# The gate's products before the pair products, their sums in the bank of the keys by values: linear attention and a balanced mixture of experts on one core

## The chip, the cores and the metric

The kernel runs on one core of a Trainium2 chip, as one launch. The metric is the device time of that core in microseconds (us). Inputs and outputs are float32 in device memory.

## The reference

An attention block without softmax (RWKV-5 form: 4 batches, 8 heads, 768 steps, 48 values a head) feeds a layer of eight experts in which every expert gets the same number of tokens.

```python
for t in range(S):
    cur = einsum('bhd,bhe->bhde', u * k_t, v_t)
    y[:, :, t] = einsum('bhd,bhde->bhe', r_t, state + cur)
    state = w * state + einsum('bhd,bhe->bhde', k_t, v_t)
x = y as (B*S, H*D) = (3072, 384)
logits = x @ w_gate                     # 8 experts
order = argsort(-logits.flatten())      # greedy: the best (token, expert) first,
                                        # at most 384 tokens an expert
out[mask_e] = relu(x[mask_e] @ w1[e]) @ w2[e]
```

## The kernel before, in words

The program has two parts: the attention (about the first 127 us) and the experts. The change lies in the attention, class `Mild`, in which the order of the work is written out by hand: each engine executes its instructions in the order in which the code issues them, and waits for another engine only where data or a buffer has to come free.

**Rounds.** The 768 steps are cut into C = 6 chunks of 128, and a unit n is one chunk of one batch, 24 units in all, batches innermost (unit n has batch n % 4 and chunk n // 4). `run` (from L619) has a loop of 24 rounds; round n issues, in this order:

- loads for later units (SP's queue, L336);
- `turn(n + 2)` (L480): TensorE turns the scaled keys and the receptances of unit n+2 (L458, tiles `kT_ps` and `rT_ps`); ScalarE copies the keys out (L475) and VectorE multiplies the receptances by powers of the decay (L477);
- `rows((n - 1,), "few")` (L607): TensorE turns the finished x of unit n-1 back into rows (L595, tile `x_ps` in the bank "few"), ScalarE copies them (L604), SP writes them to memory (L605);
- `diagonal(n + 2, ...)` (L487): ScalarE writes the diagonals of the matrices AT of unit n+2, eight multiplications, four a half (L495). In rounds 1 and 2, and in those with a gate, the second half comes later;
- in rounds 3 and 4 only, `keep(n - 1)` here; in later rounds keep belongs to `outputs`;
- `pairs(n + 1)` (L497): 16 products of keys and receptances inside the chunk (L505, 32 records in the trace, tile `g_ps`), then two masked copies by VectorE into AT (L512);
- `keys(n + 3)` (L436) and `own(n + 3)` (L442, L443): three multiplications on GpSimd (POOL);
- in rounds 4, 8, 12, 16 and 20 (`full`), `gate(n // 4 - 1, ...)`: the logits of the chunk that was just finished, for all four batches at once, and the second half of the diagonal;
- `outputs(n)` (L534): products of the receptances with the states (L545, `y_ps<-rT,states`); `keep(n)` (L514) except in the last chunk: keys by values (L524, tile `kv_ps` in the bank "counts"), which VectorE adds to the state (L529; in the first chunk it multiplies them into it, L532) and GpSimd then scales (L530); the products by AT (L545, `y_ps<-AT,vts`); in rounds with a gate `logits` (L582), which turns the sums of the gate (L585, tile `lt_ps` in "few") and copies them into LG (L586); and ScalarE's copy of the result (L564).

**The gate** (L568 to L580): for each of 4 row groups of x and each of 4 batches one product of 128 rows by 32 columns, each batch in column group 32b of one PSUM tile, `lg_ps`; 16 products, 32 records (L575). ScalarE then copies the sums to `lg` (L580). The last chunk's gate runs behind the loop (L728, L730).

**PSUM.** The eight banks are handed out by tags, one buffer each. The tags that matter: "few" is used by turn after turn of small things (x_ps, lg_ps, lt_ps, and most of the small products of the assignment); "counts" belongs in the loop to kv_ps alone. A new tile of a tag waits until every reader of the tile before has finished.

**Work placed between.** `step(n, ...)` calls pieces of the early assignment (from round 17, L886) that pick an expert with few tokens and list them before the attention is over: the list's products go to "few" too (L1201 to L1205), their sums and comparisons run on VectorE (L936 and around). None of its places in rounds with a gate is used. `chores` are constants, on VectorE and GpSimd.

The few lines of the loop that set the order around the change:

```python
                if n + 1 < N:
                    self.pairs(n + 1, lambda: step(n, "products"))
                step(n, "paired")
            if n + 3 < N:
                self.keys(n + 3)
                self.own(n + 3)
            if full:
                self.gate(n // B - 1, range(B))
                if n + 2 < N:
                    self.diagonal(n + 2, halves[1])
```

Of the kernel before, what the change touches and what calls it, by code (L numbers as in the profile page):

```python
# [10 lines left out]
F32 = mybir.dt.float32  # L11
# [10 lines left out]
T = 128  # L22
# [4 lines left out]
def attention_any(ctx, tc, r, k, v, w, u, wg, x_dram, LG, ident, walk):  # L27
# [237 lines left out]
    for n in range(len(units)):  # L265
        if n + 1 < len(units):
            scale(n + 1)
        pairs(n)
        if n > 0:
            gate(n - 1)  # L270
        outputs(n)
    gate(len(units) - 1)


class Mild:
# [292 lines left out]
    def gate(self, c, bs):  # L568
        nc, HP, B = self.nc, self.HP, self.B
        if c not in self.lgs:  # L570
            self.lgs[c] = self.walk.ps.tile([128, T], F32, name="lg_ps", tag="few")
        lg_ps = self.lgs[c]
        for o in range(HP):
            for b in bs:
                nc.tensor.matmul(lg_ps[32 * b:32 * b + 32, :], self.wgp[:, o, :], self.xts[c * B + b][:, o, :],  # L575
                                 start=(o == 0), stop=(o == HP - 1), skip_group_check=True,
                                 tile_position=(0, 32 * b))
        if B - 1 in bs:
            self.lg = lg = self.pool.tile([128, T], F32, name="lg", bufs=1)
            nc.scalar.copy(lg, lg_ps)  # L580
# [38 lines left out]
    def run(self, step):  # L619
        N, B, C, walk = self.N, self.B, self.C, self.walk  # L620
        self.live = {n: {} for n in range(N)}
        self.start()
        u_ps = self.spread_u()
        self.again_one(0, 0)
        k0 = self.keys_turned(0, True)
        self.again_one(0, 1)
        self.idle(2, "g_ps")
        r0 = self.r_turned(0)
        self.copy_u(u_ps)
        self.own(0)  # L630
        self.scaled(0, "k", k0, "pieces")
        self.scaled(0, "r", r0, "pieces")
        self.table(self.WK, "k")
        self.again_one(1, 0)
        self.table(self.WR, "r")
        self.again_one(1, 1)
        self.idle(2, "g_ps")
        k1 = self.keys_turned(1, True, walk.ps, "few")
        wk_ps = self.wk_turned()
        r1 = self.r_turned(1, walk.ps, "counts")  # L640
        self.wk_table(wk_ps)
        self.scaled(1, "k", k1, self.WK)
        self.own_sum(0)
        self.diagonal(0, (0,))
        self.again_one(2, 0)
        self.diagonal(0, (1,))
        self.again_one(2, 1)
        self.scaled(1, "r", r1, self.WR)
        self.own(1)
        self.keys(0)  # L650
        self.own_sum(1)
        nc, AB = self.nc, self.ones8
        nc.vector.tensor_mul(self.chunk, AB[:, 0, :, 1, 8], AB[:, 0, :, 1, 8])
        self.pairs(0)
        self.diagonal(1)
        self.own(2)
        chores = walk.constants()
        for n in range(N):
            self.load(n + 5, "kr")
            self.load(n + 4, "v")  # L660
            if n == 2:
                self.gate_weights()
            soon, split, full = n <= B, 0 < n < 3, n >= B and n % B == 0
            halves = ((0,), (1,)) if split or full else ((0, 1), ())
            if n == 0:
                self.turn(2, True)
                self.own_sum(2)
                self.idle(3, "y_ps")
                self.pairs(1)
                self.keys(1)  # L670
            else:
                step(n, "first")
                if not soon and n + 3 < N:
                    self.again(n + 3)
                if n == 2:
                    self.own_sum(n + 2)
                if split:
                    self.keep(n - 1)
                    self.pairs(n + 1)
                if n + 2 < N:  # L680
                    if n != 2 and n + 3 < N:
                        self.own_sum(n + 2)
                    self.turn(n + 2, between=lambda: step(n, "turning"))
                if n <= N - B:
                    self.rows((n - 1,), "few")
            if soon:
                self.again_one(n + 3, 0)
            if n + 2 < N:
                self.diagonal(n + 2, halves[0])
            if soon:  # L690
                self.again_one(n + 3, 1)
            if n > 2:
                step(n, "turned")
                if n <= B:
                    self.keep(n - 1)
                if n + 1 < N:
                    self.pairs(n + 1, lambda: step(n, "products"))
                step(n, "paired")
            if n + 3 < N:
                self.keys(n + 3)  # L700
                self.own(n + 3)
                if n == 1:
                    self.keys(2)
            if full:
                self.gate(n // B - 1, range(B))
                if n + 2 < N:
                    self.diagonal(n + 2, halves[1])
            if n == N - 1:
                rows = self.rows_turned((N - 4, N - 3), "g_ps", lambda: step(n, "rows"))
                self.rows_out((N - 4, N - 3), rows)  # L710
            self.outputs(n, lambda: step(n, "states"), (lambda: self.logits(n // B - 1)) if full else (lambda: None))
            if split:
                self.diagonal(n + 2, halves[1])
            if n == N - 4:
                self.own_sum(N - 1)
            step(n, "last")
            if n == 13:
                walk.guess_most(self.LG[:, 0:3 * B, :], AX.XY)
            if n == 14:
                walk.guess(walk.ps.tile([128, 128], F32, name="most_ps", tag="few"), self.ident)  # L720
            if n == N // 2 + 1:
                for _ in chores:
                    pass
                self.test()
            if n > 2:
                for _ in range(6):
                    next(chores, None)
        self.gate(C - 1, range(B - 1))  # L728
        one = self.rows_turned((N - 2,), "kT_ps")
        self.gate(C - 1, [B - 1])  # L730
        last = self.rows_turned((N - 1,), "g_ps")
        self.logits(C - 1)
        return one, last
# [1285 lines left out]
```

## Time and profile before

| | us |
|---|---|
| median of 3 runs | 394.56 (394.26 to 394.99) |
| the profiled execution, time | 393.36 |
| the profiled execution, span from first to last instruction | 391.6 |
| TensorE busy (matmul) | 377.2 |
| VectorE busy | 281.4 |
| ScalarE busy | 169.3 |
| GpSimd busy | 141.2 |

All rows come from that one profiled execution. PE is the matmul stream of TensorE, PEld its weight loads, DVE VectorE, ACT ScalarE, POOL GpSimd, SP the queue that issues loads and stores. A busy time of PE is modelled at its ends, so steps on PE are read here from the start of one group to the start of the next. In a timeline row the first number is the start of a group of like instructions, the second the time from the first one's start to the last one's end. What stands in brackets at the end is idle time of that engine just before the row, and who ended it; "issue" means that nothing which the profile shows was waited for.

### The profile page before, as it was taken

The page shows a single profiled execution, that of the slowest core. Times are in us where ns is not written, and L with a number is a line of the kernel's source. Part 1 is how long each engine was busy: PE and PEld are TensorE (multiplying, and loading weights), DVE is VectorE, ACT ScalarE, POOL GpSimd, SP SyncE. Part 2 cuts the span into 40 slices and gives each one's busy share as a digit, 9 for nine tenths or more (in the row PEclk, how much of TensorE's full clock was granted, in tenths as well). Part 3 has the DMA queues.
Part 4 walks back from the last instruction along what each step waited for, and adds up shares of the span by engine and source line. Part 5 has one row for each costly group of instructions (what it writes and reads, how often), then busy time and mean ns, then how long its engine had stood idle before and what let it go on. Part 6 is the DMA issues. An engine that isn't in the chain of part 4 may idle for free. (4 is left out here: it accounts for less than half of the span.)

```text
span 391.6 us, 9858 instructions
## 1 busy us (share of the span) xinstructions
PE 377.2 (96%) x3777; PEld 306.2 (78%) x3777; DVE 281.4 (72%) x959; ACT 169.3 (43%) x452; POOL 141.2 (36%) x173
## 2 busy tenths in 40 slices
PE   8899999999999999999999999999999999999992
PEld 7677888888877866687578899558657889989991
DVE  6755777586885788985949949888378976994530
ACT  4997989888883311312222242121222234234220
POOL 7878887767732022032122021203203212070020
PEclk9999999999999999999999999999999999999997
DMA  9999999988692164651560560109209264280010
GB/s 121 160 180 174 210 189 201 174 171 157 129 338 82 43 241 181 195 190 42 164 238 28 168 251 20 41 5 345 77 20 338 85 231 173 52 329 24 2 62 27
DMA packets 95335, 57.35 MB, mean 146 GB/s; under 512 B 77232, under 2 KB 89520, under 8 KB 95280
## 3 DMA queue, kind: packets, MB, share of 16 engines
q1 hardware_dynamic: 91936, 47.21, 48.0%
q0 software_dynamic: 3104, 9.44, 7.0%
q8 instruction: 31, 0.51, 0.6%
q14 instruction: 24, 0.20, 0.2%
q10 hardware_dynamic: 240, 0.00, 0.0%
HBM read 47.20 MB, written 9.44 MB: 145 GB/s over the span
## 5 line engine op out<-in xcount | busy, mean ns | idle before, releaser
L1624 PE MATMUL h_ps<-xT,w 128*128 128x384 f32 (+1 forms) x264 | 72.6, 427 | 0.0
L495 ACT ACTIVATE AT<-ident,dd 128x128 f32<-128x128 f32 x192 | 59.6, 392 | 2.2 <-DVE dd L448 2.1
L1624 PEld LDWEIGHTS h_ps<-xT,w 128*128 128x128 f32 x264 | 42.0, 191 | 19.6 <-issue 2.2
L1518 POOL DMA_INDIRECT xg<-x_rows,tok x22 | 22.5, 1021 | 92.4 <-PE h_ps L1624 23.7
L1750 POOL DMA_INDIRECT out_dram<-o_all,to x16 | 20.8, 1299 | 85.3 <-DVE o_all L1738 22.2
L1627 ACT ACTIVATE hid<-h_ps 128x384 f32<-128x384 f32 (+1 forms) x40 | 17.9, 449 | 54.2 <-PE h_ps L1624 50.9
L512 DVE COPY_PREDICATED AT<-mask,g_ps 64x512 f32<-64x512 uint8 (+1 forms) x48 | 32.4, 723 | 11.7 <-PE g_ps L505 9.9
L1756 PE MATMUL o_ps<-w,hid 128*128 128x384 f32 x96 | 32.5, 490 | 0.0
L505 PE MATMUL g_ps<-rT,kT 48*64 48x128 f32 (+1 forms) x768 | 26.3, 255 | 1.8 <-DVE AT L512 1.0
L436 POOL TENSOR_TENSOR kss<-krs,wk 128x384 f32<-128x384 f32 x24 | 24.3, 1016 | 8.0 <-DVE krs L340 5.0
L1756 PEld LDWEIGHTS o_ps<-w,hid 128*128 128x128 f32 x96 | 17.7, 190 | 10.6 <-issue 0.5
L545 PE MATMUL y_ps<-AT,vts 128*64 128x128 f32 x384 | 25.7, 276 | 0.0
L443 POOL TENSOR_TENSOR rk<-rk,u_bc 128x384 f32<-128x384 f32 x24 | 24.1, 1003 | 1.9
L505 PEld LDWEIGHTS g_ps<-rT,kT 48*64 48x64 f32 x768 | 20.6, 132 | 5.1 <-PE unread_ps L418 0.9
L442 POOL TENSOR_TENSOR rk<-krs 128x384 f32<-128x384 f32 x24 | 24.5, 1022 | 0.2 <-DMA krs<-in_r_dram 0.2
L545 PEld LDWEIGHTS y_ps<-AT,vts 128*64 128x64 f32 x384 | 20.6, 137 | 1.0 <-issue 0.7
L477 DVE TENSOR_TENSOR rT<-rT_ps,WR 112x512 f32<-112x512 f32 x23 | 15.7, 683 | 4.2 <-PE rT_ps L458 4.2
L448 DVE TENSOR_REDUCE dd<-rk 128x8 f32<-128x384 f32 x24 | 13.1, 545 | 6.9 <-POOL rk L443 6.9
L564 ACT COPY x<-y_ps 128x512 f32<-128x512 f32 x24 | 14.1, 586 | 5.9 <-PE y_ps L545 5.0
L458 PE MATMUL rT_ps<-ident,krs 128*112 128x128 f32 x96 | 15.4, 281 | 0.5 <-DMA krs<-in_r_dram 0.4
L1698 PE MATMUL pa_ps<-T,S 128*128 128x192 f32 x80 | 15.8, 331 | 0.0
L1729 PE MATMUL p_ps<-W,H 128*128 128x128 f32 x128 | 15.8, 275 | 0.0
(340 smaller groups left out, 834.2 us busy)
## 6 DMA issues: line engine op xcount, KB each, us to landing
w<-in_moe_w_dram SPq DMA_DIRECT2D x18, 1536.0 KB, 8.7
krs<-in_k_dram SPq DMA_DIRECT2D x24, 192.0 KB, 4.5
krs<-in_r_dram SPq DMA_DIRECT2D x24, 192.0 KB, 4.8
vts<-in_v_dram SPq DMA_DIRECT2D x24, 192.0 KB, 4.9
x_rows<-xr SPq DMA_DIRECT2D x24, 192.0 KB, 3.5
xg<-x_rows,tok POOLq DMA_INDIRECT x22, 4.0
out_dram<-o_all,to POOLq DMA_INDIRECT x16, 2.7
out_dram<-o_sb,to POOLq DMA_INDIRECT x5, 4.7
```

The costliest lines, as they stand in the source:

```text
L436: self.nc.gpsimd.tensor_mul(self.kss[:, n % self.NS].rearrange("p (g h) d -> p g h d", g=2)[:, :, :, 0:D], src, self.wk.rearrange("p (g h) ...
L442: nc.gpsimd.tensor_mul(rk, self.krs[:, n % self.NK, 1, 0:H, 0:D], self.krs[:, n % self.NK, 0, 0:H, 0:D])
L443: nc.gpsimd.tensor_mul(rk, rk, self.u_bc)
L495: nc.scalar.mul(AT[:, z, a, :], self.ident, dd[:, h:h + 1])
L505: nc.tensor.matmul(g_ps[ts(i, PD), z, a, i * PD:], kT[rows, a, ts(i, PD)], rT[rows, a, i * PD:], start=True, stop=True)
L512: nc.vector.copy_predicated(out=AT[keys, :, :, steps], mask=mask, data=g_ps[keys, :, :, steps])
L545: nc.tensor.matmul(yv[q * PD:(q + 1) * PD, o // 2, o % 2, :], lhsT, rhs, start=(o // 2, q) not in seen, stop=stop, skip_group_check=True)
L1518: nc.gpsimd.indirect_dma_start(out=xg[:, c, :], out_offset=None, in_=x_dram[0:within, :], in_offset=bass.IndirectOffsetOnAxis(ap=tok[:, c: ...
L1624: nc.tensor.matmul(h_ps[j][:, at], w1[:, f, ts(j, 128)], xT[:, f, at], start=(f == 0), stop=(f == KD - 1))
L1627: nc.scalar.activation(hid[:, j, 0:m], h_ps[j][:, 0:m], AF.Relu)
L1750: nc.gpsimd.indirect_dma_start(out=to, out_offset=bass.IndirectOffsetOnAxis(ap=tok, axis=0), in_=o_sb, in_offset=None)
L1756: nc.tensor.matmul(o_ps, hid[:, j, ts(c, 128)], w2[:, j, :], start=(j == 0), stop=(j == KF - 1))
```

## The change

The call of the gate (with the second half of the diagonal behind it) moves from behind `pairs`, `keys` and `own` to ahead of `pairs`, within the same round. The gate's sums of the first five chunks are held in the bank "counts" instead of "few"; those of the last chunk stay in "few".

```diff
         if c not in self.lgs:
-            self.lgs[c] = self.walk.ps.tile([128, T], F32, name="lg_ps", tag="few")
+            self.lgs[c] = self.walk.ps.tile([128, 512], F32, name="lg_ps", tag="counts" if c < self.C - 1 else "few")
+            self.lgs[c] = self.lgs[c][:, 0:T]
         lg_ps = self.lgs[c]
...
                 if n <= B:
                     self.keep(n - 1)
+                if full:
+                    self.gate(n // B - 1, range(B))
+                    if n + 2 < N:
+                        self.diagonal(n + 2, halves[1])
                 if n + 1 < N:
                     self.pairs(n + 1, lambda: step(n, "products"))
                 step(n, "paired")
...
-            if full:
-                self.gate(n // B - 1, range(B))
-                if n + 2 < N:
-                    self.diagonal(n + 2, halves[1])
```

## Rows read from the trace of the kernel before

**Rows 1.** The page, part 1: busy time, share of the span, instructions.

```profile
PE 377.2 (96%) x3777; PEld 306.2 (78%) x3777; DVE 281.4 (72%) x959; ACT 169.3 (43%) x452; POOL 141.2 (36%) x173
```

**Rows 2.** Busy time by stretch: stretch, length, engines (instructions), granted clock, DMA share, GB/s.

```profile
90.00:120.00 30.00, 29.04 (x630) 24.38 (x624) 23.61 (x68) 23.10 (x68) 15.86 (x19) 1.00 0.74 191
```

**Rows 3.** Timeline, PE, round 10 (ordinary): start, length, engine, line, operation.

```profile
61.65 0.97 PE L505 MATMUL g_ps<-rT,kT 48*64 48x128 f32 x29
62.36 0.33 PE L545 MATMUL y_ps<-rT,states 48*64 48x128 f32 x2
...
63.11 0.67 PE L524 MATMUL kv_ps<-vts,kss 128*64 128x48 f32 x16
```

**Rows 4.** Timeline, round 8 (with a gate): PE, then DVE, then ACT.

```profile
51.06 0.55 PE L595 MATMUL x_ps<-ident,x 112*128 112x112 f32 x4
51.54 1.10 PE L505 MATMUL g_ps<-rT,kT 48*64 48x128 f32 x32
52.57 1.08 PE L575 MATMUL lg_ps<-x,wgp 128*32 128x128 f32 x32
53.58 0.67 PE L545 MATMUL y_ps<-rT,states 48*64 48x128 f32 x16
54.18 0.67 PE L524 MATMUL kv_ps<-vts,kss 128*64 128x48 f32 x16
...
49.69 0.32 DVE L529 TENSOR_TENSOR states<-states,kv_ps 128x192 f32<-128x192 f32 x1
...
52.78 1.36 DVE L512 COPY_PREDICATED AT<-mask,g_ps 64x512 f32<-64x512 uint8 x2 [0.36 <-PE g_ps L505]
...
53.72 0.27 ACT L580 COPY lg<-lg_ps 128x128 f32<-128x128 f32 x1 [0.41 <-PE lg_ps L575]
```

**Rows 5.** Timeline, weight loads (PEld), round 8: the gate and the state products.

```profile
52.57 0.81 PEld L575 LDWEIGHTS lg_ps<-x,wgp 128*32 128x32 f32 x32 [0.17 <-issue]
53.58 0.43 PEld L545 LDWEIGHTS y_ps<-rT,states 48*64 48x64 f32 x16 [0.20 <-issue]
```

**Rows 6.** Timeline, PE, behind the loop: rows turned, the last gate's last batch, rows turned.

```profile
124.26 0.60 PE L595 MATMUL x_ps<-ident,x 112*128 112x112 f32 x4
124.79 1.06 PE L575 MATMUL lg_ps<-x,wgp 128*32 128x128 f32 x8
125.78 0.60 PE L595 MATMUL x_ps<-ident,x 112*128 112x112 f32 x4
```

**Rows 7.** Timeline, round 4: PE's keys by values (keep(3), then keep(4)), DVE's read.

```profile
31.95 0.67 PE L524 MATMUL kv_ps<-vts,kss 128*64 128x48 f32 x16
...
35.35 0.67 PE L524 MATMUL kv_ps<-vts,kss 128*64 128x48 f32 x16
...
32.67 0.36 DVE L532 TENSOR_TENSOR states<-kv_ps,chunk 128x192 f32<-128x192 f32 x1
```

**Rows 8.** Timeline, round 20: PE, then DVE.

```profile
108.60 0.55 PE L595 MATMUL x_ps<-ident,x 112*128 112x112 f32 x4
109.20 1.10 PE L505 MATMUL g_ps<-rT,kT 48*64 48x128 f32 x32
...
111.83 1.09 PE L545 MATMUL y_ps<-AT,vts 128*64 128x128 f32 x16
112.86 0.33 PE L585 MATMUL lt_ps<-ident,lg 128*128 128x128 f32 x1
...
107.72 1.33 DVE L512 COPY_PREDICATED AT<-mask,g_ps 64x512 f32<-64x512 uint8 x2
...
110.07 0.35 DVE L529 TENSOR_TENSOR states<-states,kv_ps 128x192 f32<-128x192 f32 x1
```

**Rows 9.** Timeline, rounds 21 and 22: PE's list product and pairs(23); DVE.

```profile
113.76 0.25 PE L1203 MATMUL e_some_ps<-e_vals,e_row 128*128 128x32 f16 x4
...
117.96 0.94 PE L505 MATMUL g_ps<-rT,kT 48*64 48x128 f32 x29 [0.69 <-DVE e_upto L1172]
...
114.06 0.55 DVE L448 TENSOR_REDUCE dd<-rk 128x8 f32<-128x384 f32 x1 [1.20 <-POOL rk L443]
...
114.53 0.18 DVE L936 TENSOR_TENSOR e_some<-e_some_ps,quarter 128x32 f32<-128x32 f32 x1
```

## The prediction

> **What bounds the kernel now.** I read the page first: TensorE (PE) is busy 377.2 us, 96% of the span [rows 1]. The table by stretch then says how tight the stage of the change is: in the loosest 30 us of those that hold gates, 90 to 120 us, PE is still busy 29.04, at full granted clock, VectorE (DVE) 23.61 [rows 2]. So a round costs what PE's queue costs, and a wait put into that queue is lost unless PE waits later anyway. Third, PE's timeline of an ordinary round (n = 10) and of one with a gate (n = 8), start against start [rows 3, 4]. Fourth, the idle gaps of the weight loads, which show what a change of product shape costs [rows 5]. Last, the two rounds in which the bank of the keys by values (tag "counts") is read late, n = 4 and n = 20 [rows 7, 8], and what follows round 20 [rows 9].
>
> **What moves.** The diff moves two calls, but only PE's order changes. Between the old place and the new one the loop issues pairs(n+1) (PE, then DVE's two masked copies), and on POOL one keys and two own products; the step "paired" has no entry in a round with a gate. ACT issues nothing there, so its order (first half of the diagonal, copy of the gate's sums, second half) stays, and DVE, POOL and SP keep theirs. Every instruction count stays. What changes: in rounds 4, 8, 12, 16 and 20 the gate's 32 product records stand ahead of the 32 of the pairs; the gate must wait until "counts" has been read out, and the next keep until ACT has copied the gate's sums.
>
> **The gain, rounds 8, 12 and 16.** In the old order x (rows turned) starts at 51.06, pairs 51.54, gate 52.57, state products 53.58, keys by values 54.18: 3.12 us [rows 4]. In an ordinary round pairs to keys by values takes 63.11 - 61.65 = 1.46, and only 29 of 32 pair records stand ahead of the first state product [rows 3]: the two have one shape (48 rows, 64 columns) and overlap. The round with a gate pays 1.03 + 0.60 = 1.63 for them. There the gate costs the weight loads two gaps, 0.17 and 0.20 [rows 5]; ahead of the pairs it costs one of these, and the step from turning to pairs becomes one from turning to gate. The two steps that the trace lacks are bounded by neighbours. Turning to gate: 124.79 - 124.26 = 0.53 at the end of the stage [rows 6]; from below, what turning to pairs takes, 0.48 [rows 4]. Gate to pairs: gate to state products, which have the pairs' shape, 1.01 [rows 4]; from below, gate to turning, 0.99 [rows 6]. New sum: 0.48 to 0.53, plus 0.99 to 1.01, plus 1.46, so 2.93 to 3.00. The gain is 0.12 to 0.19 a round; I take 0.15, the middle: three rounds -0.45 (-0.36 to -0.57).
> The waits that come with it are hidden there. In round 8 the bank's last reader, the state's sum, ends at 49.69 + 0.32 = 50.01 [rows 4], 1.5 us before the gate could start. ACT's copy of the sums had waited 0.41 for the gate before 53.72 [rows 4]; with the gate 1.03 earlier it comes that 0.41 earlier and ends at 53.58, ahead of the keep at 54.03. DVE's masked copies, which began at 52.78, come 1.0 later, and the state's sum behind them a little later than before; the readers of that state come four rounds on.
>
> The Trainium skill ("TensorEngine Tiling (Array Packing)", Key Properties) says that changing the tiling mode, not just the tile, drains the engine; the gaps agree in kind. "TensorE: Matmul & The Clock Gate" of the Trainium skill (Part 2) puts the drain at about 128 cycles, 53 ns at 2.4 GHz, so as an estimate by that figure the three rounds would gain 0.16 in all; the rows, 0.17 to 0.20 a gap, decide.
>
> **The price, round 4.** This is the one round in which keep(n-1) stands right before the new place. Its products start at 31.95, and DVE reads them out from 32.67 to 33.03 [rows 7]; until now PE went on with the pairs in that time, and the gate will wait for it. From DVE's end to the product takes 0.15 in round 20 (masked copy until 107.72 + 1.33 = 109.05, pairs at 109.20 [rows 8]). So gate 33.18, pairs 34.19, keys by values 34.19 + 1.46 = 35.65 against 35.35 [rows 7]: +0.30. Bounds: +0.15 if the hand-over costs nothing, +0.47 if a gap of 0.17 comes on top. No later wait of PE gives that back: the stretch up to 120 us hardly has any [rows 2].
>
> **The price, round 20.** DVE is late here: the early assignment's work stands ahead of the sum that reads the bank of keep(19), which runs only from 110.07 to 110.42 [rows 8]. The gate, free to go at 108.60 + 0.48 = 109.08, waits until 110.42 + 0.15 = 110.57. Pairs follow at 111.58, and the products by AT (there is no keep in this round) 1.46 later, 113.04, against 111.83 [rows 8]: 1.21 late. What of it arrives? Three paths lead to pairs(23), at 117.96, which had waited 0.69 us for DVE [rows 9]. First, DVE's masked copy of round 20: pairs to copy takes 52.78 - 51.54 = 1.24 [rows 4], so it starts at 112.82 and ends about 1.33 later, 114.15; DVE had idled 1.20 us for POOL until 114.06 [rows 9], so 0.09 comes through. Second, the early list's product uses the bank "few" behind the turned logits. These come at 113.04 + 1.03 = 114.07, and they and the four turnings behind them take five times 0.12 (0.48 for four, [rows 4]), so the list product starts at 114.67, lasts 0.25 and is read at about 114.95 instead of 114.53 [rows 9]: 0.42 late, in a chain of DVE that has no gap from there to the masked copy that releases pairs(23). Third, PE itself comes 0.9 late (114.67 against 113.76), within its 0.69 of waiting plus the 0.42. I take +0.42, the largest; bounds +0.09 and the whole 1.21.
>
> The Trainium skill ("PSUM — Partial Sum Buffer", PSUM bank collisions) has PSUM guarded by bank and quadrant, not by address: a rule against this change, since the gate writes all four quadrants of a bank that DVE still has to read. The pairs that start only behind the masked copy [rows 8] agree.
>
> **Sum.** -0.45 + 0.30 + 0.42 = +0.27 us. The profiled execution took 393.36 (span 391.6), 1.2 below the median of the runs, 394.56; so 393.63 there, and 394.8 beside the median. A measurement of this kernel can tell about 0.2%, 0.79 us, from no change, and the sum lies within that. Its bounds without the whole price of round 20: -0.57 + 0.15 + 0.09 = -0.33 to -0.36 + 0.47 + 0.42 = +0.53, so 394.2 to 395.1.
>
> **The rivals.**
> B, pure gain. With the bank free in time in rounds 4 and 20, all five rounds gain 0.15, and round 20 also the 0.12 for which its pairs waited for DVE (109.08 to 109.20): -0.87, 393.7, faster. It needs the read of keep(3) over before 32.5 and that of keep(19) before 109; the rows have them 0.5 and 1.4 us later [rows 7, 8], and the diff moves nothing on DVE ahead of either.
> C, slower: round 20 pays in full. The place is the gate's wait for the sum at 110.07, the price 1.21 for 0.42: -0.45 + 0.30 + 1.21 = +1.06, 395.6. It decides if the list product comes over 0.7 us later than I put it, so that DVE's chain moves by the whole delay. For it: logits, bank "few", list product and DVE follow each other without slack. Against it: the 1.20 for which DVE idled and the 0.69 for which PE did [rows 9].
> D, the change does not save a drain: the steps into and out of the gate cost as much together as what goes away. Then three rounds gain nothing, and round 4 loses 0.15 more: 0.30 + 0.15 + 0.42 = +0.87, 395.4. The step of 0.53 [rows 6] speaks against it, but no row has a gate before pairs.
>
> **Chances.** The forecast 0.70: all of its bounds lie within 0.2%. B 0.08, faster. C 0.13, slower. D 0.09, at the edge: 0.05 slower, 0.04 same. Together faster 0.08, same 0.74, slower 0.18. The range takes the forecast's bounds, 0.2 more below for the spread of the runs (394.26 to 394.99), and reaches up over D and C: 394.0 to 395.7. It leaves out B and little else.
>
> **What would show it.** In rounds 8, 12 and 16: x to keys by values about 2.97 for 3.12, pairs to keys by values 1.46. In round 4 a wait of about 0.6 before the gate, which starts near 33.2, behind DVE's read. In round 20 PE waits about 1.5 us before the gate for DVE's sum, the products by AT come 1.2 late against the round's start and pairs(23) 0.4 late. From 128 us on all is shifted by about 0.3. The forecast is wrong if no wait stands before the gates of rounds 4 and 20, if gate to pairs is far from 1.0, or if the shift at the end of the attention is not that at the end of the kernel.

## The result and the profile after

The changed kernel takes 395.48 us (median of 13 runs, 394.94 to 396.27) against 394.56 (13 runs of the kernel before, 394.26 to 394.99): ratio 1.0022, 95% interval 1.0013 to 1.0030, so 0.92 us slower. In a second session it was 395.51 against 394.84, ratio 1.0018 (1.0010 to 1.0027), 0.67 slower. Both intervals leave out 1. The loss is about the 0.2% which the prediction took for the limit of what can be told; it has the sign of the predicted sum (+0.27) and two and a half to three and a half times its size.

PE's waits, longest in total, of the kernel after (engine and line that waited, releaser, us in total, times, longest; lines from the gate on are one higher than before, so L576 is the gate):

```profile
PE lg_ps L576 <- DVE states L529: 1.3, 1, 1.3
PE g_ps L505 <- DVE AT L512: 1.0, 2, 0.7
...
PE lg_ps L576 <- DMA wgp<-in_moe_w_gate_dram: 0.7, 1, 0.7
...
PE g_ps L505 <- DVE e_upto L1173: 0.4, 1, 0.4
```

The gate now waits twice: for DVE's state sum, as forecast, and for a DMA, the load of its own weights, of which the prediction had said nothing.

First the gain. The timeline of PE, kernel after, rounds 8 and 12:

```profile
51.69 0.60 PE L596 MATMUL x_ps<-ident,x 112*128 112x112 f32 x4
52.22 1.08 PE L576 MATMUL lg_ps<-x,wgp 128*32 128x128 f32 x32
53.23 0.97 PE L505 MATMUL g_ps<-rT,kT 48*64 48x128 f32 x29
53.94 0.33 PE L545 MATMUL y_ps<-rT,states 48*64 48x128 f32 x2
...
54.70 0.67 PE L524 MATMUL kv_ps<-vts,kss 128*64 128x48 f32 x16
...
70.40 0.55 PE L596 MATMUL x_ps<-ident,x 112*128 112x112 f32 x4
70.88 1.08 PE L576 MATMUL lg_ps<-x,wgp 128*32 128x128 f32 x32
71.89 0.97 PE L505 MATMUL g_ps<-rT,kT 48*64 48x128 f32 x29
...
73.36 0.67 PE L524 MATMUL kv_ps<-vts,kss 128*64 128x48 f32 x16
```

Against [rows 4]: turning to gate 0.53 and 0.48, gate to pairs 1.01, pairs to keys by values 1.47. From x to keys by values it is 3.01 and 2.96 (round 16: 2.96) where it was 3.12. Only 29 of the 32 pair records now stand ahead of the first state product, as in an ordinary round [rows 3]. The weight loads of the kernel after, round 8, against [rows 5]:

```profile
52.22 0.81 PEld L576 LDWEIGHTS lg_ps<-x,wgp 128*32 128x32 f32 x32
53.23 0.84 PEld L505 LDWEIGHTS g_ps<-rT,kT 48*64 48x64 f32 x31 [0.20 <-issue]
```

Around the gate one gap of 0.20 is left where there were two.

Round 4 of the kernel after, PE, then DVE, against [rows 7]:

```profile
31.57 0.60 PE L596 MATMUL x_ps<-ident,x 112*128 112x112 f32 x4 [0.16 <-ACT x L564]
32.10 0.67 PE L524 MATMUL kv_ps<-vts,kss 128*64 128x48 f32 x16
33.50 1.08 PE L576 MATMUL lg_ps<-x,wgp 128*32 128x128 f32 x32 [0.73 <-DMA wgp<-in_moe_w_gate_dram]
34.51 0.97 PE L505 MATMUL g_ps<-rT,kT 48*64 48x128 f32 x29
...
35.98 0.67 PE L524 MATMUL kv_ps<-vts,kss 128*64 128x48 f32 x16
...
32.82 0.36 DVE L532 TENSOR_TENSOR states<-kv_ps,chunk 128x192 f32<-128x192 f32 x1
```

From x to keys by values it takes 35.98 - 31.57 = 4.41. The gate starts 0.32 after DVE has read the bank (its L532 ends at 33.18), so the bank is no longer what holds it.

Round 20 of the kernel after and what follows, PE, then DVE, against [rows 8, 9]:

```profile
108.81 0.55 PE L596 MATMUL x_ps<-ident,x 112*128 112x112 f32 x4
110.68 1.08 PE L576 MATMUL lg_ps<-x,wgp 128*32 128x128 f32 x32 [1.32 <-DVE states L529]
111.69 0.97 PE L505 MATMUL g_ps<-rT,kT 48*64 48x128 f32 x29
...
113.15 1.09 PE L545 MATMUL y_ps<-AT,vts 128*64 128x128 f32 x16
...
114.78 0.25 PE L1204 MATMUL e_some_ps<-e_vals,e_row 128*128 128x32 f16 x4
...
118.51 0.95 PE L505 MATMUL g_ps<-rT,kT 48*64 48x128 f32 x29 [0.38 <-DVE e_upto L1173]
...
110.27 0.35 DVE L529 TENSOR_TENSOR states<-states,kv_ps 128x192 f32<-128x192 f32 x1
...
112.93 1.34 DVE L512 COPY_PREDICATED AT<-mask,g_ps 64x512 f32<-64x512 uint8 x2 [1.13 <-PE g_ps L505]
114.26 0.55 DVE L448 TENSOR_REDUCE dd<-rk 128x8 f32<-128x384 f32 x1
115.07 0.19 DVE L937 TENSOR_TENSOR e_some<-e_some_ps,quarter 128x32 f32<-128x32 f32 x1 [0.26 <-PE e_some_ps L1204]
```

Read against the round's x: the products by AT come at +4.34 (they came at +3.23), 1.11 late; pairs(23) at +9.70 (+9.36), 0.34 late. DVE's 1.20 of waiting for POOL has gone into its 1.13 of waiting for the pairs, and the list product is what passes the rest on, with 0.26 of waiting on DVE.

The trace pair shows 1.8 us between the spans (393.4 and 391.6), twice what the runs show. 0.55 of it are there at pairs(23) (118.51 against 117.96). Another 0.73 are a stall behind round 23 that kernels of either order show or lack (see the last section). The rest, about 0.5, lies in the experts, whose part of the span, from LG's last copy on, takes between 264.9 and 265.8 us in the 13 profiles of this case without regard to the order.

### The profile page after: what moved, and what is told of

It reads as the page before. It is cut to its first block, busy times and chain, and to the rows that moved or that the text cites. A ratio compares the mean times of both kernels' runs of the same rounds, so it can differ in the third digit from the quotient of the medians.

```text
span 393.4 us, 9853 instructions
## 1 busy us (share of the span) xinstructions
PE 377.2 (96%) x3777; PEld 306.5 (78%) x3777; DVE 281.6 (72%) x959; ACT 168.7 (43%) x452; POOL 141.6 (36%) x173
## 4 chain that ended last, share of the span: by engine, by line
PE 73%; DVE 11%; issue 8%; DMA 3%; POOL 1%; ACT 1%; POOLq 0%; SPq 0%; another core or an unknown queue 0%; DVEq 0%
PE h_ps L1625 14%; PE pa_ps L1699 7%; PE o_ps L1757 7%; PE y_ps L545 6%; PE g_ps L505 5%; PE h_ps L1602 4%; PE pb_ps L1699 3%; PE hb_ps L1602 3%; PE e_h_ps L1850 3%; PE kT_ps L458 3%; PE x_ps L596 2%; PE kv_ps L524 2%; PE rT_ps L458 2%; PE lg_ps L576 2%; DVE AT L512 2%
## 5 line engine op out<-in xcount | busy, mean ns | idle before, releaser
L545 PE MATMUL y_ps<-rT,states 48*64 48x128 f32 x320 | 16.0, 276 | 0.0
```

What stands on the lines that cost most here:

```text
L545: nc.tensor.matmul(yv[q * PD:(q + 1) * PD, o // 2, o % 2, :], lhsT, rhs, start=(o // 2, q) not in seen, stop=stop, skip_group_check=True)
```

## Experiments

Each is timed against the kernel before in the same session. The first four ran on one chip (number 8 on record), the next four on another (6), the last three on a third (7). "x to kv" is the time from the rows turned to the keys by values of a round, start to start, read from the trace. "+9.70" and the like count from x of the same round 20. The code edits are against the changed kernel, unless it is said otherwise; lines left out are marked by three points.

**The changed kernel again.**

> The changed kernel itself, a second profile. Theory S (the stall of 0.7 us at 124 to 126 us, in which PE's last gate record and ACT's copy of the last result both start late, belongs to this program): the trace shows it again, and the time is 0.8 to 1.0 us above the kernel before. Theory N (the stall belongs to that one execution): it is gone, the copy into LG of the last chunk comes about 0.5 us after that of before instead of 1.3, and what lifts the median by 0.92 beyond the sum of rounds 4, 8, 12, 16 and 20 (about +0.4) must lie behind the attention.

395.51 against 394.84, ratio 1.0018: 0.67 slower, a little less than theory S said. The stall was there again, as in all four kernels of that session, also in the one whose order is that of before (the bank alone); all four have counts, so the kernel before itself was profiled later (below). Round 4, PE then DVE, shows what the first profile hid:

```profile
31.17 0.60 PE L596 MATMUL x_ps<-ident,x 112*128 112x112 f32 x4 [0.16 <-ACT x L564]
31.70 0.67 PE L524 MATMUL kv_ps<-vts,kss 128*64 128x48 f32 x16
32.88 1.08 PE L576 MATMUL lg_ps<-x,wgp 128*32 128x128 f32 x32 [0.51 <-DVE states L532]
...
35.36 0.67 PE L524 MATMUL kv_ps<-vts,kss 128*64 128x48 f32 x16
...
32.42 0.36 DVE L532 TENSOR_TENSOR states<-kv_ps,chunk 128x192 f32<-128x192 f32 x1
```

Here the weights were in time, and DVE alone held the gate, 0.10 beyond its end: 4.19 from x to kv, not 4.41.

**Rounds 8, 12 and 16 alone.**

```diff
-            self.lgs[c] = self.walk.ps.tile([128, 512], F32, name="lg_ps", tag="counts" if c < self.C - 1 else "few")
+            self.lgs[c] = self.walk.ps.tile([128, 512], F32, name="lg_ps", tag="counts" if c in (1, 2, 3) else "few")
...
-                if full:
+                if full and n in (8, 12, 16):
                     self.gate(n // B - 1, range(B))
...
+            if full and n not in (8, 12, 16):
+                self.gate(n // B - 1, range(B))
+                if n + 2 < N:
+                    self.diagonal(n + 2, halves[1])
```

> The new order and the bank counts in rounds 8, 12 and 16 alone; rounds 4 and 20 as before. My theory (each of the three gains 0.11 to 0.16, nothing else moves): 0.4 us faster than before, pairs(23) 0.4 us earlier against the start of round 4. Rival (the saved drain comes back later in the chain through DVE from round 17 on): same as before within 0.1.

394.37 against 394.84, ratio 0.9990 (0.9982 to 0.9999): 0.47 faster. x to kv is 2.96, 2.96 and 2.95; round 4 takes 3.77 and pairs(23) comes at +9.35, as before. From x of round 4 to pairs(23) it is 85.88, where the second profile of the kernel before (below) has 86.34: the 0.46 gained in the three rounds are still there at the end of the loop.

**Rounds 4, 8, 12 and 16.** The same edit with (4, 8, 12, 16), and counts for c in (0, 1, 2, 3).

> The new order in rounds 4, 8, 12 and 16; round 20 as before. If round 20 is the main price: the loss of round 4 (about 0.48) and the gain of the three (0.43) cancel, within 0.2 us of before, and the stall of 1.3 us before the gate of round 20 is gone. If the main price lies elsewhere (a stall at the end of the attention that comes with any shift): 0.4 to 0.7 us slower than before.

395.34 against 394.84, ratio 1.0012 (1.0003 to 1.0020): 0.50 slower, though no wait stands before the gate of round 20. So round 20 is not the main price. Nor is it a stall that comes with any shift, since rounds 8, 12 and 16 alone gained. What is left is round 4, and its row in this profile (PE) says so:

```profile
34.01 1.08 PE L576 MATMUL lg_ps<-x,wgp 128*32 128x128 f32 x32 [1.10 <-DMA wgp<-in_moe_w_gate_dram]
```

x to kv is 4.78 there, 1.01 above the 3.77 of the kernel with rounds 8, 12 and 16 alone.

**The bank alone.** The gate behind the pairs as before, its sums in counts in all five rounds. Against the kernel before:

```diff
-            self.lgs[c] = self.walk.ps.tile([128, T], F32, name="lg_ps", tag="few")
+            self.lgs[c] = self.walk.ps.tile([128, 512], F32, name="lg_ps", tag="counts" if c in (0, 1, 2, 3, 4) else "few")
+            self.lgs[c] = self.lgs[c][:, 0:T]
```

> The gate where it was, its sums in counts in all five rounds. My theory (the bank costs only where its reader is late): rounds 4, 8, 12, 16 unchanged, the gate of round 20 waits about 0.35 us for DVE's state sum that ends near 110.42 (it would start at 110.22), and the time is 0.1 to 0.4 us above before. Rival (the bank costs nothing by itself, the order does): same as before within 0.1, no wait before any gate.

394.75 against 394.84, ratio 1.0002 (0.9993 to 1.0011): no difference that can be told. Round 20, PE then DVE:

```profile
108.80 1.10 PE L505 MATMUL g_ps<-rT,kT 48*64 48x128 f32 x32
110.07 1.08 PE L576 MATMUL lg_ps<-x,wgp 128*32 128x128 f32 x32 [0.18 <-DVE states L529]
...
109.67 0.35 DVE L529 TENSOR_TENSOR states<-states,kv_ps 128x192 f32<-128x192 f32 x1
```

The wait for DVE is there (the gate 1.27 after the pairs instead of 110.22 - 109.20 = 1.02), shorter than the 0.35 expected, but pairs(23) comes at +9.36 as before: the 0.25 does not arrive. Neither theory has it whole. In this kernel the bank costs something only where the gate is also early.

**The kernel before again.**

> The kernel before itself, a second profile. In the first one the copy into LG of the last chunk came 8.67 us after pairs(23); in the changed kernel and in all three variants it comes 9.38 to 9.52 after, with PE's last gate records and ACT's copy of the last result late together. Theory N (the first profile of before was a lucky execution, 1.2 us under its median, and the late end of the attention belongs to every program): 9.4 here too, and round 4 takes 3.77 to 3.95 from x to keys by values. Theory S (the late end comes with the bank counts for the gate's sums): 8.7 again.

393.54 against 393.50 on another chip, ratio 1.0001. Round 4 takes 3.77. LG's last copy comes 8.68 after pairs(23), and 8.66 to 8.68 also in the three changed kernels beside it, two of which have counts. So the late end of the attention belongs to no program, and both theories fall as they were put. What is left is the chip or the session; each session ran on one chip, so these two are not told apart.

**Rounds 8, 12, 16 and 20.** The edit with (8, 12, 16, 20), and counts for c in (1, 2, 3, 4).

> The new order and counts in rounds 8, 12, 16 and 20; round 4 as before. If round 4 is the larger price (0.4 to 1.0 us by the three profiles of it) and round 20 costs 0.35 at pairs(23): 0.43 gained, 0.35 lost, within 0.2 us of before. If round 20 is the larger: 0.5 us or more slower.

393.38 against 393.50, ratio 0.9998 (0.9986 to 1.0010): no difference that can be told, as expected. The gate of round 20 waits 1.32 us again, and pairs(23) comes at +9.71, 0.35 late. With the gain of rounds 8, 12 and 16 at 0.4 to 0.5 the medians put round 20 at about 0.3, within wide intervals.

**The gate's weights loaded a round earlier.**

```diff
-            if n == 2:
+            if n == 1:
                 self.gate_weights()
```

> The changed kernel with the gate's weights loaded one round earlier. Theory D (the gate of round 4 waits for its weights, which land at about 33.4, as well as for DVE's read of the bank): its wait falls to that for DVE alone, x to keys by values 4.15 to 4.25 in every execution, the time 0.1 to 0.3 us below the changed kernel and still 0.2 to 0.5 above before. Rival (only DVE holds it): the same as the changed kernel, 4.2 to 4.8.

393.85 against 393.50, ratio 1.0013 (1.0003 to 1.0023): 0.35 slower. The weights now land before 30 us. Round 4, PE then DVE:

```profile
31.70 0.60 PE L596 MATMUL x_ps<-ident,x 112*128 112x112 f32 x4 [0.16 <-ACT x L564]
...
33.36 1.08 PE L576 MATMUL lg_ps<-x,wgp 128*32 128x128 f32 x32 [0.46 <-DVE states L532]
...
35.84 0.67 PE L524 MATMUL kv_ps<-vts,kss 128*64 128x48 f32 x16
...
32.95 0.36 DVE L532 TENSOR_TENSOR states<-kv_ps,chunk 128x192 f32<-128x192 f32 x1
```

x to kv is 4.14, with DVE the only wait, 0.05 from its end to the gate. In the trace the two causes are apart: the bank costs 4.14 - 3.77 = 0.37, the weights what comes on top: 0.05 at most in the profile with 4.19, where DVE alone held the gate, and up to 0.64 in the others above and below (4.27, 4.41, 4.78). By the times alone the difference from the changed kernel (0.35 against 0.67 and 0.92, on other chips) is not settled; the intervals overlap.

**The order alone.** The gate ahead of the pairs in all five rounds, its sums in few (`c in ()` holds for no chunk).

```diff
-            self.lgs[c] = self.walk.ps.tile([128, 512], F32, name="lg_ps", tag="counts" if c < self.C - 1 else "few")
+            self.lgs[c] = self.walk.ps.tile([128, 512], F32, name="lg_ps", tag="counts" if c in () else "few")
```

> The gate ahead of the pairs in all five rounds, its sums in few, the bank of the rows just turned. Each gate must wait for ACT's copy of those rows, which in round 8 ends 1.07 us after the turning starts: gate 1.2 after x instead of 0.5, x to keys by values 3.66 instead of 3.12 or 2.96, in rounds 8, 12 and 16; round 20 waits 0.7 instead of 1.3. My theory: 1.4 to 2.5 us slower than before. Rival (the copy is done sooner than PE gets there): as the changed kernel without the waits of rounds 4 and 20, 0.4 to 0.8 us faster than before.

395.57 against 393.50, ratio 1.0054 (1.0036 to 1.0071): 2.1 us slower. PE's waits, then round 8, then the gate of round 4:

```profile
PE lg_ps L576 <- ACT xr L605: 2.3, 4, 0.6
...
51.72 0.58 PE L596 MATMUL x_ps<-ident,x 112*128 112x112 f32 x4
52.88 1.08 PE L576 MATMUL lg_ps<-x,wgp 128*32 128x128 f32 x32 [0.57 <-ACT xr L605]
...
33.54 1.08 PE L576 MATMUL lg_ps<-x,wgp 128*32 128x128 f32 x32 [0.61 <-DMA wgp<-in_moe_w_gate_dram]
```

x to kv is 3.63, 3.59, 3.59 in rounds 8, 12, 16. So the order needs the other bank: without it the gates of rounds 8, 12, 16 and 20 each wait 0.57 for ACT's copy of the rows. In round 4, where keep(3) stands between, ACT is no wait; the weights are, and x to kv is 4.30 with the bank of keep(3) out of play.

**Round 4 alone.** The edit with (4,), and counts for c in (0,).

> The new order and counts in round 4 alone. If the wait for bank and weights there is carried to the end: x to keys by values 4.15 to 4.8 instead of 3.77, and the time 0.4 to 1.0 us above before. Rival (a wait that early is given back by a later wait of PE or DVE): the same as before within 0.1.

394.27 against 393.49, ratio 1.0022 (1.0011 to 1.0034): 0.78 slower. x to kv is 4.27, the gate held 0.59 by its weights. Nothing later gives it back: LG's last copy comes at 127.31, 0.53 later than in the second profile of the kernel before, though x of round 4 was 0.05 earlier. By the medians this one round costs as much as the whole change (0.67 and 0.92); what the other four rounds gain and lose is smaller.

**Rounds 8, 12 and 16 once more, and a version with round 4.** The first is the kernel of above. The second has the new order in (4, 8, 12, 16), counts for c in (1, 2, 3) only, and the weights loaded at n == 1.

> Rounds 8, 12 and 16 alone, once more, beside the next kernel: 0.4 to 0.5 us below before.

> Rounds 8, 12 and 16 with counts as in the kernel beside it; round 4 also in the new order, but with its sums in few, where keep(3) stands between the copy of the rows and the gate and hides that wait, and with the gate's weights loaded one round earlier; round 20 as before. My theory: x to keys by values of round 4 is 3.6 to 3.7 instead of 3.77, the time 0.5 to 0.6 us below before. Rival (the earlier load of the weights delays the loads behind it on the queue, or ACT's copy comes later than the keep): no better than the kernel beside it, or up to 0.5 us slower than that.

393.12 and 393.11 against 393.49: ratios 0.9999 (0.9982 to 1.0016, which settles nothing by itself) and 0.9989 (0.9979 to 0.9999). Round 4 of the second kernel takes 3.64 from x to kv, as expected, with no wait of PE at its gate: keep(3) stands between ACT's copy and the gate. Beside the 4.30 of the order alone, this shows the load by itself: both have the new order and few in round 4, and the early load takes 0.66 away. The 0.13 below 3.77 does not show in the time: 0.38 faster, not the 0.5 to 0.6 expected, and no better than the kernel beside it. Rounds 8, 12 and 16 alone is the smaller edit of the two, faster than the kernel before by the interval of the earlier session (0.9982 to 0.9999) and by the median of this one. On the chip where it ran in one session with the changed kernel the medians are 394.37 and 395.51.

## Why the prediction was right or wrong

The time came out within the range (395.48 in 394.0 to 395.7), but 0.7 above the predicted 394.8 and above the forecast's own bounds, which end at 395.1. The range held it only because it was stretched up to take in the rivals C and D, and neither of these is what happened. So the sign and most of the steps were right, while the hit of the range was luck. Step by step:

- **The gain, rounds 8, 12 and 16**: -0.45 forecast. The rows give 0.11, 0.16 and 0.16, so -0.43, and rounds 8, 12 and 16 alone ran 0.47 and 0.37 faster by the medians. Turning to gate took both ends of the forecast's step (0.53 in round 8, 0.48 in the other two), and gate to pairs is the 1.01 of gate to state products. The 0.53 is not the gate's: with round 4 alone moved, round 8 has the old order and takes 0.54 from turning to pairs, and 3.17 in all. Rival D falls: the step that it denied is saved.
- **The price, round 20**: +0.42 forecast at pairs(23). The rows give 9.70 - 9.36 = +0.34, and the runs about +0.3 (0.12 faster with round 20, 0.37 to 0.47 without). Of the three paths the list product is the one that passes time on, as put: it is read at +6.26 instead of +5.93, 0.33 late. By DVE's masked copy nothing comes through (0.09 forecast): it ends against the next sum without a gap, and this starts at +5.45 instead of +5.46. PE's own lateness stays inside its wait, which shrank from 0.69 to 0.38. The rows put this wait down to DVE's `e_upto`, right behind the masked copy that the prediction named. Rival C falls: 0.8 of the 1.1 were absorbed.
- **The price, round 4**: +0.30 forecast, with an upper bound of 0.47. This is the step that failed. It said of the gate that it will wait for DVE's read of the bank, and priced that alone. That part is 0.37 (4.14 - 3.77, with the weights early). Missing was the second thing that the first gate of the kernel waits for, its weights, a term put at nothing without a reason: they are asked for only in round 2, and the gate, moved about 1 us forward (free to start 1.13 after x instead of 2.16), overtook them. With counts and the new order in round 4, x to kv is 4.19, 4.27, 4.41 and 4.78 in four profiles with the late load, and 4.14 in one with the early load; with few it is 4.30 late and 3.64 early. Round 4 alone costs 0.78 us in the runs.
- **The hand-over from DVE to PE** of 0.15 was too long: 0.05 to 0.10 in round 4 and 0.06 in round 20 (110.62 to 110.68). It is about the 0.08 by which round 20 was cheaper. The bank's 0.37 in round 4 is the forecast 0.30 with 0.17 more for the starting value and 0.10 less for this.
- **Rival B** falls by the waits of rounds 4 and 20 in the table of waits.

The failed step was to be seen beforehand. In the trace of before, the loads of the weights, then round 4 of PE:

```profile
L404 SPq DMA_DIRECT2D wgp<-in_moe_w_gate_dram x2: 434/623/812, 28.4 to 29.3; - x2
...
DMA to landing us min/median/max: 4.3/4.7/5.0
...
31.41 0.60 PE L595 MATMUL x_ps<-ident,x 112*128 112x112 f32 x4 [0.16 <-ACT x L564]
...
33.75 1.08 PE L575 MATMUL lg_ps<-x,wgp 128*32 128x128 f32 x32
```

The two pieces landed at 28.4 + 5.0 = 33.4 and 29.3 + 4.3 = 33.6 (paired the other way, the second would land at 34.3, behind the gate that reads it). So the gate could not start at the forecast 33.18: it stood at 33.75 already, in its old place. With 33.75 the prediction's own steps give pairs at 34.76 and keys by values at 36.22, so +0.87 for round 4 and +0.84 for the sum, an estimate for that execution, against the 0.92 and 0.67 measured. The starting value was off with it: x to kv is 3.94 there, against 3.77 in the five other profiles that have the old order in round 4, and the 0.17 lie in front of the gate (1.20 from pairs to gate; 1.02 in the second profile of the kernel before).

With the measured terms the sum is +0.78 - 0.42 + 0.30 = +0.66 by the runs, against +0.92 and +0.67 measured for the change. The traces have one step that holds all five rounds and ends ahead of the stall, from x of round 4 to pairs(23). It is 86.34 in the second profile of the kernel before (86.37 with the bank alone, on the chip with the stall), 85.88 and 85.89 with rounds 8, 12 and 16, 86.24 with round 20 added to these, 86.93 with round 4 alone, and 86.94 and 86.72 in the changed kernel: -0.45 for the three rounds, +0.35 for round 20, +0.59 for round 4, and +0.60 and +0.38 for the whole. That is 0.3 less than the medians of the same sessions show. The two profiled executions were faster than these medians (395.17 and 394.67 against 395.48 and 395.51), and round 4 differs by up to 0.6 from one execution to the next; that this is the whole of the rest is not shown.

The last sign that the prediction named, a shift at the end of the attention equal to that at the end of the kernel, cannot be read: the stall and the experts' spread of 0.9 us are both larger than the shift.

## What to carry to other kernels

When an instruction is moved forward, list everything that it reads, not only the buffer that the change touches: an operand whose load used to land unseen just before its old place is a new wait at the new one, and the first use in a loop is where to look. A saved change of product shape is worth about 0.15 us here, so one late reader of a borrowed bank (0.37 in round 4, 0.35 in round 20) outweighs two of them. Move the step only in the rounds where both bank and operands are free, which the trace of before already shows. And where a range is stretched to cover rivals, a time inside it says little of the mechanism: read the steps.

## What was not expected

The first profile of the changed kernel and all four profiles of chip 8, whatever the order, show a stall of about 0.7 us behind round 23; the first profile of the kernel before and all seven of chips 6 and 7 do not. The changed kernel's second profile, PE then ACT:

```profile
124.72 0.29 PE L576 MATMUL lg_ps<-x,wgp 128*32 128x128 f32 x1 [0.33 <-issue]
...
124.80 0.59 ACT L564 COPY x<-y_ps 128x512 f32<-128x512 f32 x1 [2.27 <-remote]
```

PE's last record of these and ACT's copy start late together, and the trace puts neither wait down to a line ("issue" and "remote"). In the kernel before, second profile, the copy starts inside the gate's 24 records:

```profile
123.40 1.07 PE L575 MATMUL lg_ps<-x,wgp 128*32 128x128 f32 x24
...
123.53 0.59 ACT L564 COPY x<-y_ps 128x512 f32<-128x512 f32 x1 [0.78 <-PE y_ps L545]
```

From pairs(23) to LG's last copy it is 9.38 to 9.52 us on the one chip and 8.66 to 8.68 on the two others; the medians of the kernel before were 394.84 there and 393.50 and 393.49 on these, so the stall is about half of their difference. What causes it was not tried. It matters for reading: the profile of before was of the second kind (8.67; its execution took 393.36, less than any of the 13 runs timed beside the changed kernel) and that of after of the first (9.40), so a comparison of these two traces alone would have put 0.7 us too much to the change.
